# An attention-plus-MLP kernel on one core: prologue, load order and wave placement changed

## The chip, the cores and the metric

One Trainium2 chip, of which the program uses one core. The metric is device microseconds of one execution. Matmuls run on PE (TensorE); DVE (VectorE), ACT (ScalarE) and POOL (GpSimd) do the rest; SP (SyncE) issues most of the DMAs.

## The reference

Polynomial-sketch attention, and then an MLP with a swish whose slope is a parameter of each hidden unit. Batch 4, 4 heads, 1088 tokens, 32 numbers per head; r = 8, so a token has 64 features per head; 4352 tokens in all, d_model 128, d_ff 2048.

```python
def phi(x):
    a = np.einsum('rd,bhsd->bhsr', S1, x)
    b = np.einsum('rd,bhsd->bhsr', S2, x)
    return np.einsum('bhsi,bhsj->bhsij', a, b).reshape(*x.shape[:-1], r * r)
q_p, k_p = (phi(q), phi(k))
kv = np.einsum('bhsf,bhsd->bhfd', k_p, v)
z = np.sum(k_p, axis=2)
num = np.einsum('bhsf,bhfd->bhsd', q_p, kv)
den = np.einsum('bhsf,bhf->bhs', q_p, z)[..., None] + 1e-06
x = (num / den), heads side by side            # 4352 x 128
h = x @ w_in
g = h * (1.0 / (1.0 + np.exp(-beta * h)))
out = g @ w_out
```

## The kernel before

The kernel folds beta into the weights: `winp` is w_in times beta, `woutp` is w_out over beta, both in f16, so that the swish is a plain Silu on ACT. They are made on the chip: `scale_w_in` (POOL, eight pairs of 128-column blocks), `scale_w_out` (ACT, first half) and `scale_w_out_pool` (POOL, second half). `beta_rows` spreads beta over the partitions with matmuls against ones.

Each batch is an `Attention` object. Its steps: `k_turn` and `q_turn` (DVE 32x32 transposes of the loaded k and q, to kT and qT), `k_project` and `q_project` (PE, both sketches at once, then the DVE transposes back to `ab`), `k_product` (outer product of the two sketches, split between DVE and POOL), `v_copy`, `kv` (PE, key features against v with a column of ones, so z comes with it), `kv_spread`, `weights`, `kv_repeat` (layouts for the next products), `denominators`, `q_multiply` and `q_back` (query features of one third of the tokens, transposed to `qpt`), and `num` (PE, query features against kv, four token groups s on 32 rows each). Batch 0 divides after num (`num_first`, `spread_rden`, `rden_rows`, `quotient`); the others scale the query features first (`weigh`), and then `num_part` and `evacuate` write `xT`, the MLP's input in f16.

The MLP goes over three chunks of a batch (384, 384 and 320 columns), each in 8 waves. A wave is two matmuls with `winp` into a pair of PSUM banks, one Silu over both to `gT`, and, two waves later, the two matmuls of `second` with `woutp` that add to `acc`. So there are 24 waves per batch and 96 in all. After a chunk's last one the DVE transposes `acc` to `osb` and SP stores it.

The order on each engine is the order in which the code is written. A list of slots (`at_wave`) says behind which wave which attention step of the same or the next batch is issued. Every engine takes its instructions in that order, so an instruction that waits holds up what stands behind it. PSUM tiles come from three tags with two buffers each: `att` (a bank), `acc` (a bank), `wave` (a pair).

All loads are issued at the start of the program: k of batch 0 and beta from ACT's queue, the rest from SP's in the order S1, S2, q, v of batch 0, w_in, w_out, then k, v, q of batches 1, 2, 3. `warm(n)` issues n matmuls on zeros.

Of the kernel before, what the change touches and what calls it, by code (L numbers as in the profile page):

```python
# [13 lines left out]
P = 128  # L14
T = 32
# [3 lines left out]
def kernel(  # L19
# [61 lines left out]
    def load_v(b):  # L81
        for s in range(NS):
# [23 lines left out]
    load_v(0)  # L106
    nc.scalar.dma_start(out=betat, in_=moe_beta.rearrange("(p j) -> p j", j=NJ))
    nc.sync.dma_start(out=w_in_sb, in_=moe_w_in)
    nc.sync.dma_start(out=w_out_sb, in_=moe_w_out.rearrange("(p j) m -> p j m", j=NJ))
    for b in range(1, B):  # L110
        nc.sync.dma_start(out=k_in[b], in_=k_rows[b])
        load_v(b)
        nc.sync.dma_start(out=q_in[b], in_=q_rows[b])
# [109 lines left out]
    def scale_w_in():  # L223
        for j in range(0, NJ, 2):
# [25 lines left out]
    class Attention:  # L250
# [68 lines left out]
        def kv(self, r):  # L319

            if r == 0:
                self.kvp = bank("att")
            for c in range(C):
                for g in range(4):
                    h = 2 * r + g // 2
                    nc.tensor.matmul(  # L326
                        out=self.kvp[T * g : T * g + T, r * (D + 1) : (r + 1) * (D + 1)],
                        lhsT=self.kp[:, c * H + h, (g % 2) * T : (g % 2) * T + T],
                        rhs=self.vc[:, c, h, :],
                        start=(c == 0),  # L330
                        stop=(c == C - 1),
                    )

        def kv_spread(self):
            kvx = sb.tile([P, 4, 2, D], F32, tag="kvx", name="kvx")
            nc.vector.tensor_tensor(
                out=kvx,
# [344 lines left out]
```

## Time and profile before

| | us |
|---|---|
| three runs | 134.78, 133.62, 134.84; median 134.78 |
| the profiled execution | 135.82, of which the span is 134.1 |
| PE busy / weight loads | 113.0 / 62.0 |
| ACT busy | 83.5 |
| DVE busy | 69.4 |
| POOL busy | 29.8 |
| mean granted PE clock | 0.955 |
| DMA read / written | 8.80 MB / 2.23 MB |

The span runs from the first instruction to the last. The chain of waits is followed back from the last instruction, at each step to what released it; "issue" in it is time in which an engine waited for nothing that the profile shows. PE's busy time counts matmuls whose ends are modelled, so a busy PE need not be at its peak. In a row of the timeline stand start, duration, engine, line, operation, tiles, shapes and count, and in brackets the idle time before it with its releaser. The granted clock has records only from about 16 us on; before that the profile shows 1.00.

### The profile page before, as it was taken

To read this page: it belongs to the slowest core of one execution; us is meant where nothing else is said; L and a number is where in the kernel's file an instruction comes from. 1 tells how busy PE (TensorE), PEld (TensorE's weight loads), DVE (VectorE), ACT (ScalarE), POOL (GpSimd) and SP (SyncE) were. 2 spreads that over 40 slices of the span, in tenths; PEclk is the share of its full clock that TensorE was granted. 3 is DMA by queue.
4 is the path that set the end of the run, shared out by engine and by line. 5 is a ranking of instruction groups with operands and counts; after the bars stand their busy time and mean duration, and the time that the engine had idled before them with its cause. 6 is when DMAs were issued, how large, how long until landed. Compare 5 with 4: busy or idle time off the path is not lost.

```text
span 134.1 us, 4076 instructions
## 1 busy us (share of the span) xinstructions
PE 113.0 (84%) x1777; PEld 62.0 (46%) x1777; DVE 69.4 (52%) x131; ACT 83.5 (62%) x141; POOL 29.8 (22%) x48
## 2 busy tenths in 40 slices
PE   6986950579996999975999998999999899999940
PEld 2312530453643675643446644645574565555610
DVE  4429640338589312999950379988036991010110
ACT  1354210076753757864767786877878689999930
POOL 6205899910005700000191000008000000000000
PEclk9999999555999999999999999999999999999997
DMA  4999999999981210013300301321030031203222
GB/s 144 223 175 289 403 160 191 223 177 250 156 187 61 42 29 0 2 19 45 48 6 5 59 0 19 45 39 15 5 50 13 0 59 17 37 12 49 34 40 39
DMA packets 22122, 11.29 MB, mean 84 GB/s; under 512 B 18773, under 2 KB 20821, under 8 KB 21849
## 3 DMA queue, kind: packets, MB, share of 16 engines
q1 hardware_dynamic: 21808, 10.46, 39.3%
q10 hardware_dynamic: 296, 0.57, 1.3%
q8 instruction: 14, 0.23, 0.7%
q14 instruction: 4, 0.02, 0.1%
HBM read 8.80 MB, written 2.23 MB: 82 GB/s over the span
## 4 chain that ended last, share of the span: by engine, by line
PE 52%; DVE 20%; ACT 12%; DMA 6%; issue 5%; SPq 0%; DVEq 0%; ACTq 0%
PE wave L556 15%; ACT gT L559 11%; PE acc L536 11%; PE att L442 7%; DMA q_in<-in_q_dram 6%; PE att L326 5%; DVE qp L425 4%; DVE qpt L433 4%; PE att L286 3%; PE att L469 3%; PE att L381 3%; PE acc L180 2%; DVE qT L265 2%; PE att L366 2%; DVE kp L312 1%
## 5 line engine op out<-in xcount | busy, mean ns | idle before, releaser
L559 ACT ACTIVATE gT<-wave 128x768 f16<-128x768 f32 (+1 forms) x96 | 68.5, 775 | 21.5 <-PE wave L556 21.3
L556 PE MATMUL wave<-xT,winp 128*128 128x384 f16 (+1 forms) x192 | 46.2, 323 | 2.2 <-DVE xT L512 1.4
L536 PE MATMUL acc<-gT,woutp 128*128 128x384 f16 (+1 forms) x192 | 45.3, 318 | 0.2 <-ACT gT L559 0.2
L556 PEld LDWEIGHTS <-winp 128*128 128x128 f16 x192 | 16.6, 99 | 20.6 <-issue 10.0
L312 POOL TENSOR_TENSOR kp<-ab 128x768 f32<-128x768 f32 (+1 forms) x4 | 12.1, 3037 | 62.3 <-DVE ab L295 47.6
L536 PEld LDWEIGHTS <-woutp 128*128 128x128 f16 x192 | 18.7, 98 | 11.3 <-issue 0.7
L541 DVE STREAM_TRANSPOSE osb<-acc 128x384 f32<-128x384 f32 (+1 forms) x12 | 6.5, 540 | 24.5 <-PE acc L536 24.5
L442 PE MATMUL att<-qpt,kvw 32*32 32x96 f32 (+1 forms) x512 | 12.4, 277 | 2.2 <-DVE qpt L433 1.8
L433 DVE STREAM_TRANSPOSE qpt<-qp 128x768 f32<-128x768 f32 x12 | 11.7, 971 | 0.2
L442 PEld LDWEIGHTS att<-qpt,kvw 32*32 32x32 f32 x512 | 7.8, 104 | 7.2 <-DVE qpt L433 2.8
L381 PE MATMUL att<-qT,wc 128*32 128x288 f32 (+2 forms) x40 | 3.6, 409 | 5.8 <-issue 5.4
L425 DVE TENSOR_TENSOR qp<-an,ab 128x768 f32<-128x768 f32 x9 | 8.4, 930 | 0.1
L225 POOL TENSOR_TENSOR winp<-w_in_sb,beta_bc 128x256 f16<-128x256 f32 x8 | 8.3, 1074 | 0.5 <-DMA w_in_sb<-in_moe_w_in_dram 0.5
L390 DVE STREAM_TRANSPOSE cc<-att 128x288 f32<-128x288 f32 (+2 forms) x5 | 2.1, 423 | 12.0 <-PE att L381 12.0
L180 PE MATMUL acc<-idle 128*128 128x512 f16 x15 | 7.0, 629 | 1.3 <-DVE idle L117 1.3
L312 DVE TENSOR_TENSOR kp<-ab 128x1536 f32<-128x1536 f32 (+1 forms) x4 | 7.3, 1825 | 0.3
L295 DVE STREAM_TRANSPOSE ab<-att 128x288 f32<-128x288 f32 x16 | 6.7, 454 | 1.2 <-PE att L286 1.2
L326 PEld LDWEIGHTS att<-vc,kp 128*32 128x32 f32 x576 | 5.9, 113 | 2.7 <-issue 2.7
L286 PE MATMUL att<-qT,wab 64*32 64x288 f32 x64 | 4.3, 482 | 3.3 <-DVE ab L295 3.1
L265 DVE STREAM_TRANSPOSE qT<-q_in 128x1088 f32<-128x1088 f32 x4 | 5.1, 1279 | 3.1 <-DMA q_in<-in_q_dram 3.1
L326 PE MATMUL att<-vc,kp 128*32 128x33 f32 x576 | 6.7, 202 | 0.0
L490 ACT COPY ns<-wave 128x192 f32<-128x192 f32 x2 | 0.6, 319 | 7.6 <-PE wave L442 7.6
(71 smaller groups left out, 81.6 us busy)
## 6 DMA issues: line engine op xcount, KB each, us to landing
q_in<-in_q_dram SPq DMA_DIRECT2D x4, 544.0 KB, 8.7
v_in<-in_v_dram SPq DMA_DIRECT2D x12, 144.0 KB, 10.7
k_in<-in_k_dram SPq DMA_DIRECT2D x3, 544.0 KB, 14.4
out_dram<-osb SPq DMA_DIRECT2D x32, 48.0 KB, 1.9
w_in_sb<-in_moe_w_in_dram SPq DMA_DIRECT2D x1, 1024.0 KB
w_out_sb<-in_moe_w_out_dram SPq DMA_DIRECT2D x1, 1024.0 KB, 9.2
out_dram<-osb SPq DMA_DIRECT2D x16, 40.0 KB, 1.7
k_in<-in_k_dram ACTq DMA_DIRECT2D x1, 544.0 KB, 3.9
```

The lines of the kernel that those rows point to most:

```text
L180: nc.tensor.matmul(out=w, lhsT=idle[:, 0:P], rhs=idle, start=True, stop=True)
L225: nc.gpsimd.tensor_tensor(out=winp[:, j : j + 2, :], in0=apx(w_in_sb, j, [[1, 2], [NJ, P]]), in1=apx(beta_bc, j, [[1, 2], [NJ, P]]), op=AL ...
L265: nc.vector.transpose(out=self.qT[:, 0:U, :].rearrange("p u t -> p (u t)"), in_=q_in[self.b])
L286: nc.tensor.matmul(out=banks[p][T * s : T * s + T, 0 : C * T], lhsT=wab[64 * p : 64 * p + 64, :], rhs=apx(src[64 * p : 64 * p + 64], s * s ...
L312: eng.tensor_tensor(out=apx(self.kp, c0 * H * F, [[F, n], [R, R], [1, R]]), in0=apx(t, c0 * H * 2 * R, [[2 * R, n], [1, R], [0, R]]), in1= ...
L326: nc.tensor.matmul(out=self.kvp[T * g : T * g + T, r * (D + 1) : (r + 1) * (D + 1)], lhsT=self.kp[:, c * H + h, (g % 2) * T : (g % 2) * T ...
L425: nc.vector.tensor_tensor(out=apx(self.qp, 0, [[F, n], [R, R], [1, R]]), in0=a, in1=apx(self.ab, c0 * H * 2 * R + R, [[2 * R, n], [0, R], ...
L433: nc.vector.transpose(out=apx(self.qpt, ch * CW * T, [[T, CW], [C * T, 2 * H], [1, T]]), in_=self.qp.rearrange("p n f -> p (n f)"),)
L442: nc.tensor.matmul(out=dst[T * h : T * h + T, 0:n], lhsT=self.kvw[T * s : T * s + T, (h % 2) * 2 + fb, h // 2, :], rhs=self.qpt[T * s : T ...
L536: nc.tensor.matmul(out=acc[:, :n], lhsT=woutp[:, j, :], rhs=gT[:, j, :n], start=(j == 0), stop=(j == NJ - 1))
L556: nc.tensor.matmul(out=wave[:, jj, :n], lhsT=winp[:, j, :], rhs=x[:, :n], start=True, stop=True)
L559: nc.scalar.activation(out=gT[:, 2 * w : 2 * w + 2, :n], in_=wave[:, :, :n], func=ACTF.Silu)
```

## The change

The prologue is written in another order, with twelve idle matmuls ahead of the attention's products instead of fifteen in other places, two after `kv` and two after the first quotient. Loads other than k, q and the small ones of batch 0 are held: a memset of the target's first column, placed in the program of POOL or the DVE, must have run before SP may issue the load. w_in is held by the DVE behind the turn of k, w_out behind the k product, batch 1 by POOL between its scalings, batches 2 and 3 by the DVE 19 (k, q) and 14 (v) waves ahead of their batch's first slot wave. In batch 0 `kv` uses 64 columns at a time with its two head pairs in separate banks, half of v's copy goes from ACT to POOL, and the second and third chunk's num, denominators' rows and quotient are done together. `num` takes two token groups in turn: its matmuls alternate between two groups of 32 rows and two banks. All of w_out's scaling is on POOL, in turn with the second half of w_in's. The slots have other wave numbers.

```diff
     def load_v(b):
-        for s in range(NS):
+        for s in (0, 2, 1, 3):
...
+    def hold(eng, t):
+        eng.memset(t[:, 0:1], 0.0)
+
+    def load_w_in(eng):
+        hold(eng, w_in_sb)
+        nc.sync.dma_start(out=w_in_sb, in_=moe_w_in)
+        nc.sync.dma_start(out=betat, in_=moe_beta.rearrange("(p j) -> p j", j=NJ))
...
+    load_v_late(0, nc.gpsimd)
...
-                parts = ((nc.scalar.copy, 0, 2), (nc.scalar.copy, 2, H))
+                parts = ((nc.scalar.copy, 0, 2), (nc.gpsimd.tensor_copy, 2, H))
...
+            if self.first:
+                parts = [(nc.vector, 0, 4), (nc.vector, 4, 7), (nc.gpsimd, 7, C)]
+            else:
+                parts = [(nc.gpsimd, 6, C), (nc.vector, 0, 6)]
...
+            m = F if self.first else T
             for c in range(C):
...
+                for r in rs:
+                    for g in range(2 * F // m):
+                        h = 2 * r + g * m // F
+                        f0 = g * m % F
+                        nc.tensor.matmul(
+                            out=self.kvp[m * g : m * g + m, r * self.kvs : r * self.kvs + D + 1],
+                            lhsT=self.kp[:, c * H + h, f0 : f0 + m],
...
-        def num(self, s, dst, c0, c1):
+        def num(self, s0, banks, c0, c1):
+
             n = (c1 - c0) * T
             for fb in range(2):
                 for h in range(H):
...
+                    for i, dst in enumerate(banks):
+                        s = s0 + i
+                        nc.tensor.matmul(
+                            out=dst[T * h : T * h + T, 0:n],
+                            lhsT=self.kvw[T * s : T * s + T, (h % 2) * 2 + fb, h // 2, :],
...
+        def rden_rows(self, ch0, ch1):
+
+            banks = [bank("att") for _ in range(ch0, ch1)]
+            for i, w in enumerate(banks):
+                for s in range(NS):
...
+    warm(9)
+    a0.k_turn((0,))
+    sketches()
+    warm(2)
+    a0.k_turn((1,))
+    load_w_in(nc.vector)
+    a0.k_project()
+    a0.q_turn()
+    beta_rows()
+    warm(1)
+    a0.v_copy()
+    a0.k_product()
+    load_w_out(nc.vector)
+    a0.q_project()
+    a0.kv((0, 1))
     a0.q_multiply(0)
     a0.kv_spread()
-    a0.q_back(0)
+    warm(2)
     a0.weights()
     a0.kv_repeat()
+    a0.q_back(0)
+    nc.vector.reciprocal(out=rbetat, in_=betat)
     a0.denominators(0, 1, rz[:, 0:CW, 0:H])
-    a0.num_first(0, "wave")
+    scale_w_in(0, 4)
+    load_k(1, nc.gpsimd)
+    scale_w_in(4, 8)
+    load_q(1, nc.gpsimd)
+    a0.num_first(0, 1)
     a0.spread_rden(0, 1)
-    scale_w_out(0, NJ // 2)
-    a0.quotient(0)
-    scale_w_out_pool(NJ // 2, NJ)
+    a0.quotient(0, 1)
+    warm(2)
+    scale_w_out(0, 2)
+    load_v_late(1, nc.gpsimd)
+    for j in range(8, NJ, 2):
+        scale_w_in(j, j + 2)
+        scale_w_out(j - 6, j - 4)
+    scale_w_out(NJ - 6, NJ)
...
+            turn_k, turn_q, proj_k, proj_q, kv0, kv1, wt, den, n0, n1, n2, n3 = 0, 2, 2, 5, 7, 8, 10, 11, 18, 20, 25, 28
```

Three places show what stands in a row now. First the DVE in the prologue, from the S products to the projection of q. kT and qT are the turned k and q of batch 0, ab a projection turned back (k's, then q's), kp the k product. Before:

```order
L195 TENSOR_TENSOR wab<-att,hmask 128x32
L259 STREAM_TRANSPOSE kT_130<-k_in_70 128x576
L259 STREAM_TRANSPOSE kT_130<-k_in_70 128x512
L265 STREAM_TRANSPOSE qT_132<-q_in_66 128x1088
L574 TENSOR_REDUCE rep_161<-ident 128x32
L295 STREAM_TRANSPOSE ab<-att 128x9x32 x2
L312 TENSOR_TENSOR kp<-ab 128x1792
L295 STREAM_TRANSPOSE ab<-att 128x9x32 x2
```

The same stretch of the DVE's order after the change:

```order
L600 TENSOR_REDUCE rep_141<-ident 128x32
L277 STREAM_TRANSPOSE kT_105<-k_in_70 128x576
L218 TENSOR_TENSOR wab<-att,hmask 128x32
L277 STREAM_TRANSPOSE kT_105<-k_in_70 128x512
L109 MEMSET w_in_sb 128x1
L313 STREAM_TRANSPOSE ab<-att 128x9x32 x2
L283 STREAM_TRANSPOSE qT_107<-q_in_66 128x1088
L333 TENSOR_TENSOR kp<-ab 128x1024
L333 TENSOR_TENSOR kp<-ab 128x768
L109 MEMSET w_out_sb 128x1
L313 STREAM_TRANSPOSE ab<-att 128x9x32 x2
```

The turn of q has moved behind the first ab, and the memsets that hold w_in and w_out stand in the row.

Second, PE from kv to the first wave. Before:

```order
L326 MATMUL att<-vc_148,kp 32x33 x72
L351 MATMUL att<-zi,s2rep 128x32
L366 MATMUL att<-kvx,rep 128x256
L381 MATMUL att<-qT_132,wc 32x96 x4
L442 MATMUL wave<-qpt,kvw 32x96 x32
L469 MATMUL att<-rzt,sel_164 128x96 x4
L556 LDWEIGHTS winp
L556 MATMUL wave<-xT,winp 128x384
```

PE's order over the same steps after the change, with the idle matmuls that stand among them:

```order
L352 MATMUL wave<-vc_128,kp 64x33 x36
L203 LDWEIGHTS idle
L203 MATMUL acc<-idle 128x512
L203 LDWEIGHTS idle
L203 MATMUL acc<-idle 128x512
L376 MATMUL att<-zi,s2rep 128x32
L391 MATMUL att<-kvx,rep 128x256
L406 MATMUL att<-qT_107,wc 32x96 x4
L470 MATMUL wave<-qpt,kvw 32x96 x32
L496 MATMUL att<-rzt,sel_144 128x96 x4
```

kv has half the matmuls, each twice as wide; the steps behind it are the same, with idle matmuls ahead of `weights` and, not shown, two between the last row and the first wave.

Third, the DVE in batch 0's first waves, from the first chunk's xT on. Before:

```order
L498 TENSOR_TENSOR xT<-att,ns 128x384
L425 TENSOR_TENSOR qp<-ab 128x768
L433 STREAM_TRANSPOSE qpt<-qp 128x3x8x32
L390 STREAM_TRANSPOSE cc<-att 128x192
L392 TENSOR_TENSOR prod_154<-ab,cc 128x24x8
L399 TENSOR_REDUCE den<-prod_154 128x24
L400 RECIPROCAL rz<-den 128x6x4
L462 STREAM_TRANSPOSE rzt<-rz 128x192
L259 STREAM_TRANSPOSE kT_134<-k_in_71 128x576
L259 STREAM_TRANSPOSE kT_134<-k_in_71 128x512
L498 TENSOR_TENSOR xT<-att,ns 128x384
```

After, from the last step of the denominators on (the second and third chunk's qp and qpt stand ahead of them):

```order
L489 STREAM_TRANSPOSE rzt<-rz 128x192
L277 STREAM_TRANSPOSE kT_109<-k_in_71 128x576
L277 STREAM_TRANSPOSE kT_109<-k_in_71 128x512
L283 STREAM_TRANSPOSE qT_111<-q_in_67 128x1088
L313 STREAM_TRANSPOSE ab<-att 128x9x32 x2
L333 TENSOR_TENSOR kp<-ab 128x1536
L109 MEMSET k_in_72 128x1
L109 MEMSET q_in_68 128x1
L527 TENSOR_TENSOR xT<-att,ns 128x384 x2
L313 STREAM_TRANSPOSE ab<-att 128x9x32 x2
```

The second chunk's xT has moved behind batch 1's turn of q, projection and k product, and comes together with the third's.

More of the change, by code (lines that the diff above doesn't have):

```diff
@@ L460, in spread_rden @@
             self.rzt = sb.tile([P, 2 * CT], F32, tag="rzt", name="rzt")
-            self.rz0 = ch0
             nc.vector.transpose(out=self.rzt[:, 0:n], in_=apx(rz, ch0 * CT, [[1, n]]))
-        def rden_rows(self, ch):
-            w = bank("att")
-            for s in range(NS):
-                o = (ch - self.rz0) * CT
-                nc.tensor.matmul(
-                    out=w[:, s * CT : (s + 1) * CT],
-                    lhsT=sel4[:, s, :, :].rearrange("p h d -> p (h d)"),
-                    rhs=self.rzt[:, o : o + CT],
-                    start=True,
-                    stop=True,
-                )
-            return w
@@ L478, in num_first @@
-        def num_first(self, ch, tag):
-            self.ns = sb.tile([P, NS, CT], F32, tag="ns", name="ns")
-            for s0 in (0, 2):
-                if tag == "wave":
-                    w = pair()
-                    banks = [w[:, 0, :], w[:, 1, :]]
-                else:
-                    banks = [bank(tag), bank(tag)]
-                for i in range(2):
-                    self.num(s0 + i, banks[i], ch * CW, (ch + 1) * CW)
-                if tag == "wave":
-                    nc.scalar.copy(out=self.ns[:, s0 : s0 + 2, :], in_=w[:, :, 0:CT])
-                else:
-                    for i in range(2):
-                        nc.scalar.copy(out=self.ns[:, s0 + i, :], in_=banks[i][:, 0:CT])
@@ new lines, in num_first @@
+        def num_first(self, ch0, ch1):
+            n = (ch1 - ch0) * CT
+            self.ns = sb.tile([P, 2, NS, CT], F32, tag="ns", name="ns")
+            for s0 in (0, 2):
+                if ch0 == 0:
+                    w = pair()
+                    self.num(s0, [w[:, i, :] for i in range(2)], 0, ch1 * CW)
+                    nc.scalar.copy(out=self.ns[:, 0, s0 : s0 + 2, :], in_=w[:, :, 0:CT])
+                else:
+                    banks = [bank("att"), bank("att")]
+                    self.num(s0, banks, ch0 * CW, ch1 * CW)
+                    for i in range(2):
+                        nc.scalar.copy(
+                            out=self.ns[:, 0 : ch1 - ch0, s0 + i, :],
+                            in_=banks[i][:, 0:n].rearrange("p (c n) -> p c n", n=CT),
+                        )
@@ L502, in num_part, with quotient @@
+        def quotient(self, ch0, ch1):
+            banks = self.rden_rows(ch0, ch1)
+            x = self.xt()
+            for i, w in enumerate(banks):
+                nc.vector.tensor_tensor(
+                    out=x[:, ch0 + i, :],
+                    in0=w[:, 0:NMAX],
+                    in1=self.ns[:, i, :, :].rearrange("p s n -> p (s n)"),
+                    op=ALU.mult,
+                )
         def num_part(self, s0, ch0, ch1):
@@ L504, in num_part @@
             banks = [bank("att"), bank("att")]
-            for i in range(2):
-                self.num(s0 + i, banks[i], ch0 * CW, ch1 * CW)
+            self.num(s0, banks, ch0 * CW, ch1 * CW)
             self.parts = (s0, ch0, ch1, banks)
@@ L640 @@
+        for i, w in enumerate((n2, n3)):
+            at_wave(
+                w0 + w,
                 lambda a=a, i=i: a.num_part(2 * i, 1, NCH),
```

161 lines of the change are left out of this document (70 added, 91 removed).

## The prediction

> **What bounds the kernel now.** A measurement of this kernel tells about 1% from no change. I read the chain of waits first, then the same execution cut into five stages. The stages start at the first instruction and at waves 1, 25, 49 and 73 (a wave is two 384-column matmuls of the first MLP product; 24 waves make a batch). Columns: window, length, busy us of PE, PE weight loads, DVE, ACT and POOL, granted clock, DMA share, GB/s.
>
> ```profile
> 0.00:29.83 29.83, 19.17 (x293) 9.04 (x294) 12.39 (x31) 9.25 (x22) 18.10 (x41) 0.89 0.96 221
> 29.83:61.89 32.06, 28.13 (x496) 16.17 (x496) 21.37 (x39) 19.68 (x34) 4.31 (x3) 0.95 0.41 82
> 61.89:86.24 24.35, 23.52 (x412) 13.27 (x413) 16.62 (x30) 17.90 (x29) 4.31 (x3) 1.00 0.18 28
> 86.24:110.17 23.93, 23.43 (x413) 13.11 (x412) 16.38 (x30) 18.69 (x30) 3.08 (x1) 1.00 0.17 25
> 110.17:134.10 23.93, 18.70 (x165) 10.45 (x163) 2.66 (x5) 17.99 (x29) 0.00 (x0) 0.96 0.21 32
> ```
>
> Batches 1 and 2 keep PE busy for 97% of their time and take about 24 us each; batch 0 needs 32 us for the same number of waves; 29.8 us pass before the first wave. So the prologue and batch 0 hold what can be won. The chain in the prologue:
>
> ```profile
> 1.58 7.72 DMA q_in<-in_q_dram
> 9.33 1.31 DVE qT L265
> ...
> 11.33 1.57 PE att L286 x16
> ...
> 19.71 5.39 issue
> ...
> 25.41 1.75 PE wave L442 x57
> 27.16 1.96 PE att L469 x8
> ...
> 29.83 1.44 PE wave L556 x4
> ```
>
> Three things stand out: the k path waits for q (the DVE turns q, L265, before it takes k's projection, L295); PE stops for 5.39 us between two matmuls of one loop with nothing to wait for; and what follows is slow. The DMA view of 19.7 to 22.3 us, and then of 22.3 to 23.8 us, shows what the stop is:
>
> ```profile
> q1 hardware_dynamic: 262, 0.42, 103.2%
> ```
> ```profile
> q8 instruction: 1, 0.02, 5.8%
> ```
>
> In the stop the data queue fills all engines with loads of later batches, and the one instruction packet moves only in the second window; PE runs again at 25.1 (19.71 + 5.39). I read it as PE's next instructions arriving late. The clock follows:
>
> ```profile
> 20.00:23.40 3.40, 0.00 (x0) 0.00 (x0) 0.00 (x0) 0.00 (x0) 3.40 (x4) 0.94 1.06 186
> 23.40:26.80 3.40, 1.71 (x64) 1.42 (x64) 1.21 (x5) 0.32 (x1) 3.32 (x7) 0.50 1.04 227
> 30.10:33.50 3.40, 3.40 (x18) 1.27 (x17) 2.78 (x6) 2.15 (x3) 0.00 (x0) 0.53 1.07 249
> ```
>
> After the stop PE is granted half its clock until about 33 us.
>
> **The change, part by part.** The prologue's terms, in the order of time:
>
> ```profile
> 1.26 2.74 PE L180 MATMUL acc<-idle 128*128 128x512 f16 x6 [1.26 <-DVE idle L117]
> 4.53 1.23 PE L216 MATMUL wave<-beta,ones 1*128 1x512 f32 x3
> 4.83 1.36 DVE L259 STREAM_TRANSPOSE kT<-k_in 128x576 f32<-128x576 f32 x2
> 6.95 1.21 PE L286 MATMUL att<-kT,wab 64*32 64x288 f32 x16
> 10.81 0.83 DVE L295 STREAM_TRANSPOSE ab<-att 128x288 f32<-128x288 f32 x2
> 11.68 2.03 DVE L312 TENSOR_TENSOR kp<-ab 128x1792 f32<-128x1792 f32 x1
> 11.72 2.90 POOL L312 TENSOR_TENSOR kp<-ab 128x512 f32<-128x512 f32 x1 [7.12 <-DVE ab L295]
> 12.86 1.43 ACT L276 COPY vc<-v_in 128x448 f32<-128x448 f32 x4 [1.12 <-DMA v_in<-in_v_dram]
> 15.17 8.29 POOL L225 TENSOR_TENSOR winp<-w_in_sb,beta_bc 128x256 f16<-128x256 f32 x8 [0.54 <-DMA w_in_sb<-in_moe_w_in_dram]
> 17.32 0.42 DVE L336 TENSOR_TENSOR kvx<-att,bmask 128x256 f32<-128x256 f32 x1 [1.86 <-PE att L326]
> ```
>
> Six idle matmuls took 2.74 us, 0.46 each; nine end at 1.26 + 4.1 = 5.4. The S products lay between the end of the old six (4.0) and the beta rows (4.53): 0.5. With two more idle ones it is 6.8, and k's projection at the old 1.21 ends at 8.0 (kT, 1.36 from about 4.8, is ready). The idle matmuls lie in time that PE spent waiting; uncovered, each would cost its 0.46. Now the DVE takes ab at once: 0.83, to 8.9; then the turn of q, 1.31, to 10.2; then the k product, now in two pieces, 2.03 and 0.1 for the extra start, to 12.3. It was 13.7 before.
>
> PE meanwhile: the beta rows took from 4.53 to 6.95, 2.4, so to 10.4; one idle matmul; q's projection at the old 1.57 (the chain's row), to 12.5. The DVE now has ab of q (0.83) and qp (0.95) ahead of kvx: 14.3.
>
> On POOL its two chunks of the k product now stand behind half of v's copy. v lands when k, q and v (1.67 MB) are through: at the stage's 221 GB/s, 7.6 us, begun at about 2, so at 10 by an estimate. Half of the old ACT copy, 0.7, and 2.90 end at 13.6. Of the outer products (L326), half the instructions at twice the width, most are done by then; kv ends at about 14.1, level with the DVE. So kvx stands at 14.4 against 17.32, 2.9 earlier.
>
> From kvx to the first wave it was 29.83 - 17.32 = 12.51. The stop takes 5.39 of it. The half clock takes about half of the two PE pieces, 1.75 and 1.96; the second has a row at full clock:
>
> ```profile
> 36.19 1.03 PE L469 MATMUL att<-rzt,sel 128*128 128x96 f32 x8
> ```
>
> That is 0.9 + 0.9. What stays is 5.3. I add 0.8 for beta's reciprocal, which now stands in this chain, and for hand-overs between engines: first wave at 20.5, **9.3 us earlier**. Bounds: 18.5 if the projections and the beta rows run at half their durations and v lands at 9; 22.5 if v lands at 12.
>
> The Trainium skill ("TensorE: Matmul & The Clock Gate", Part 1) says that the default is half clock and that a busy window of some 3.4 us frees it, so nearly gapless idle matmuls from 1.3 us on should free it by about 8 us; by that the first wave would come near 19. The trace agrees on the loss (0.50 after the stop); I take the slow durations.
>
> Holding the loads adds one-column memsets (single columns, far below the rows here) and puts waits on SP: behind w_in's wait stand w_out and all of batch 1, which nothing needs earlier. POOL then owns all of w_out's scaling: eight pairs of w_in at 1.04 us (8.29 / 8) from 13.6 on, with four pairs of w_out between them that cost no more than that: the last w_in pair is ready by 26.1, and wave 8 needs it near 30. If that cover goes (v 4 us late), each microsecond counts in full. ACT loses its half of the scaling, which lay ahead of its first silu and in no chain: nothing.
>
> Batch 0. The rows that carry it:
>
> ```profile
> L433 DVE STREAM_TRANSPOSE qpt<-qp 128x768 f32<-128x768 f32 x12 | 11.7, 971 | 0.2
> L425 DVE TENSOR_TENSOR qp<-ab 128x768 f32<-128x768 f32 x3 | 2.8, 945 | 0.0
> L312 DVE TENSOR_TENSOR kp<-ab 128x1536 f32<-128x1536 f32 x3 | 5.3, 1758 | 0.3
> L498 DVE TENSOR_TENSOR xT<-att,ns 128x384 f16<-128x384 f32 x3 | 1.7, 558 | 7.1 <-PE att L469 7.1
> 32.13 0.38 DVE L390 STREAM_TRANSPOSE cc<-att 128x192 f32<-128x192 f32 x1 [0.48 <-PE att L381]
> 33.70 0.38 DVE L462 STREAM_TRANSPOSE rzt<-rz 128x192 f32<-128x192 f32 x1
> 43.99 1.79 PE att L442 x64
> 58.20 0.59 PE L442 MATMUL att<-qpt,kvw 32*32 32x96 f32 x32 [0.79 <-DVE qpt L433]
> 61.89 0.50 PE L556 MATMUL wave<-xT,winp 128*128 128x384 f16 x2 [1.39 <-DVE xT L512]
> 42.38 0.50 PE L556 MATMUL wave<-xT,winp 128*128 128x384 f16 x2
> ```
>
> Wave 9 (the second chunk) started at 42.38. In the new order the DVE sets it: two qp and two qpt (3.8), the denominators' five steps (32.13 to 34.08: 1.95), kT 1.36, qT 1.31, ab 0.83, kp 1.76, two xT 1.1: 12.1. PE's projection of q needs the two banks that xT frees, 1.0: 13.1 after the first wave, against 12.55 before, which had the slow clock but one chunk less. From there to batch 1's first wave it was 19.51; the second num_first and rden (1.79 + 1.03) have moved ahead and the two stalls (0.79, 1.39) go, because batch 1's denominators now stand eight waves ahead of the first num, not six: 14.5. Batch 0 is 27.6, and with 0.2 for one more wait of PE behind its bank 27.8, **4.3 us less**. Bounds 25.5 (PE's 28.13 busy us less 1.7 for the slow clock and 0.9 for num) and 32 (the DVE late again).
>
> Batches 1 and 2: the denominators move one wave ahead, which covers the stall of this row, and num alternates its row groups:
>
> ```profile
> 106.11 0.59 PE L442 MATMUL att<-qpt,kvw 32*32 32x96 f32 x32 [0.50 <-DVE qpt L433]
> 113.73 0.91 PE L442 MATMUL att<-qpt,kvw 32*32 32x192 f32 x32
> ```
>
> A batch has two of each: 3.0 us of num. The trace has no alternating 32-row matmul; the bounds are nothing and half of it, 1.5; I take 0.6, nearer to nothing, since 18 ns per 96-column record leave little beside issue. With the stall, 1.1 per batch, **2.2 us**. Batch 3 stays: in its stage ACT is busy 17.99 us with nothing of a next batch to move, and the rest is the way out.
>
> Sum: 9.3 + 4.3 + 2.2 = 15.8. The profiled execution took 135.82 (span 134.1), one above the median 134.78 of the three timed; the three lie within 0.9% of each other, so each must hold these waits, and I take the gain off the median: 119.0.
>
> **Rivals.** (a) The stop isn't cured. By the Trainium skill ("Runtime: NRT & Kernel Launch", Instruction fetch mechanics) instructions come in 16 KiB blocks, fetched while the block before runs, so that crossing costs almost nothing; by that the 5.39 us is something else and stays. The 0.02 MB packet that moves just before PE resumes speaks for the fetch; that other such packets cause no stop, for the page. The new kv drops 72 matmul records and num_first and rden add 72 ahead of the first wave, so the same count of instructions is reached right there, where k, q and v of batch 1 are loading. Price: 5.4 and some 2 of slow clock: 126.5. (b) The DVE chain keeps batch 0 at 32 us: 119.0 + 4.3 = 123.3; for it speaks that this chain, with 12.1 us in a row, has no slack; against it, that the stalls were at full DVE load. (c) Slower than before: the loads of batches 2 and 3 now start in waves 6 and 30 instead of being done by 42 us, so a late fetch can strike again in each stretch of full DMA. Each stop costs 5.4 plus about 3 of half clock, 8.4; the gain of 15.8 is gone with two of them, and three give 119.0 + 25.2 = 144. Against it: in batches 1 and 2, with PE 97% busy and DMA at 18%, the trace has no such stop. (d) Full clock and num halved: 119.0 - 1.5 - 1.8 = 115.7.
>
> **How the numbers follow.** Forecast, 117 to 122: 0.52. (b) and part stops, 122 to 125: 0.18. (a): 0.13. (d) and below: 0.12. (c): 0.03; ends near the old time by a mix of a and b: 0.02. The range from 115.5 to 126 leaves out half of (a), (c) and the lower end of (d), under 2 in 10. Faster 0.95, same 0.02, slower 0.03.
>
> **What would show it.** First wave at 20.5 and no issue wait of PE over 1 us before it or in waves 1 to 8; clock 1.0 from about 10 us; the k product before the end of q's projection; wave 9 at about 33.6, then batch 1 at 48; num rows of 0.91 down to about 0.7; batches 1 and 2 at 23. I'm wrong if a stop of 5 us returns, if wave 9 comes later than 16 us after the first, or if POOL's weights are late.

## The result, and the profile after

The changed kernel takes 123.65 us (median of four runs, 122.31 to 124.97) against 134.6 for the kernel before (four runs, 133.62 to 134.84). The ratio is 0.917, with a 95% interval of 0.907 to 0.926. The forecast was 119.0 with a range of 115.5 to 126: the direction and the range held, and of the 15.8 us expected 10.95 came. The profiled execution, 124.97 with a span of 123.1, is the longest of the four and the ratio leaves it out; its span is 11.0 shorter than the 134.1 of before, which is nearly the difference of the medians, so its stages serve to say where the time lies.

The stages of the changed kernel, cut at the same waves (1, 25, 49, 73). The columns are window, length, busy us of PE, PE weight loads, DVE, ACT and POOL, granted clock, DMA share, GB/s:

```profile
0.00:24.98 24.98, 19.33 (x222) 10.93 (x223) 17.48 (x34) 6.16 (x12) 14.47 (x43) 0.74 0.73 220
24.98:53.73 28.75, 27.45 (x433) 15.20 (x432) 22.85 (x42) 18.16 (x29) 12.19 (x12) 0.93 0.28 74
53.73:76.61 22.88, 22.88 (x414) 12.80 (x413) 16.63 (x33) 18.44 (x30) 4.61 (x3) 1.00 0.40 101
76.61:99.52 22.91, 22.91 (x414) 12.80 (x413) 16.38 (x30) 18.47 (x30) 3.08 (x1) 1.00 0.18 27
99.52:123.10 23.58, 18.81 (x165) 10.35 (x163) 2.58 (x5) 17.97 (x29) 0.00 (x0) 0.96 0.21 32
```

| stage | before | after | gained | forecast |
|---|---|---|---|---|
| to the first wave | 29.83 | 24.98 | 4.85 | 9.3 |
| batch 0 | 32.06 | 28.75 | 3.31 | 4.3 |
| batch 1 | 24.35 | 22.88 | 1.47 | 1.1 |
| batch 2 | 23.93 | 22.91 | 1.02 | 1.1 |
| batch 3 and the way out | 23.93 | 23.58 | 0.35 | 0 |

The prologue holds nearly all of what is missing. Its chain of waits, in order of time, has no PE stop any more, but one DVE product that stands out:

```profile
12.16 3.47 DVE qp L450
15.63 2.29 issue
```

The "issue" behind qp is no late instruction: in the DVE's timeline qp itself lasts to 18.0, and kvx stands behind it.

```profile
12.16 5.84 DVE L450 TENSOR_TENSOR qp<-ab 128x768 f32<-128x768 f32 x1
17.92 0.41 DVE L362 TENSOR_TENSOR kvx<-wave,bmask 128x256 f32<-128x256 f32 x1
```

POOL's timeline over the same time: its piece of the k product and four pairs of w_in's scaling, one behind the other without a gap, to 17.18.

```profile
11.98 1.06 POOL L333 TENSOR_TENSOR kp<-ab 128x512 f32<-128x512 f32 x1
13.01 2.12 POOL L248 TENSOR_TENSOR winp<-w_in_sb,beta_bc 128x256 f16<-128x256 f32 x2
15.13 2.05 POOL L248 TENSOR_TENSOR winp<-w_in_sb,beta_bc 128x256 f16<-128x256 f32 x2
```

PE had been done with kv for two microseconds by then, and from 12.0 on all its steps ran at half the clock (kv's 68 records 3.73, rden's eight matmuls 2.02 where a row of before has 1.03):

```profile
11.83 3.73 PE L352 MATMUL wave<-vc,kp 128*64 128x33 f32 x68 [0.35 <-POOL vc L294]
18.57 0.61 PE L376 MATMUL att<-zi,s2rep 128*128 128x32 f32 x2 [2.04 <-DVE zi L369]
22.24 2.02 PE L496 MATMUL att<-rzt,sel 128*128 128x96 f32 x8
```

The windows between the changes of the granted clock (the third column from the right):

```profile
5.20:8.60 3.40, 3.35 (x38) 1.27 (x37) 2.36 (x7) 0.61 (x2) 0.00 (x0) 1.00 1.02 239
8.60:12.00 3.40, 1.20 (x26) 0.58 (x27) 3.40 (x6) 2.35 (x4) 1.47 (x3) 1.00 0.91 294
12.00:25.60 13.60, 11.46 (x159) 8.19 (x158) 10.14 (x14) 1.01 (x3) 10.31 (x16) 0.50 0.64 202
32.40:35.90 3.50, 3.50 (x25) 1.28 (x24) 2.71 (x5) 1.78 (x4) 0.21 (x1) 0.51 0.00 0
```

The idle matmuls did free the clock, at 5.2, as the Trainium skill ("TensorE: Matmul & The Clock Gate", Part 1) let one expect; here the trace agrees (the same first nine did not free it before 13.7 in five later profiles). But in the 3.4 us from 8.6 on PE was busy for only 1.20, waiting for the DVE, and from 12.0 to 25.6 the clock was at half again.

### The profile page after: what moved, and what is told of

It reads as the page before. It is cut to its first block, busy times and chain, and to the rows that moved or that the text cites. A ratio compares the mean times of both kernels' runs of the same rounds, so it can differ in the third digit from the quotient of the medians.

```text
span 123.1 us, 3822 instructions
## 1 busy us (share of the span) xinstructions
PE 111.4 (90%) x1642; PEld 62.1 (50%) x1642; DVE 75.9 (62%) x140; ACT 79.2 (64%) x127; POOL 34.4 (28%) x58
## 4 chain that ended last, share of the span: by engine, by line
PE 69%; DVE 13%; ACT 11%; issue 3%; DVEq 0%
PE wave L587 22%; PE acc L567 19%; ACT gT L590 10%; PE att L470 8%; DVE qp L450 5%; PE att L304 4%; PE att L352 4%; PE acc L203 4%; PE att L496 3%; PE att L391 2%; PE att L406 2%; DVE kp L333 2%; DVE qpt L458 2%; DVE qT L283 1%; DVE ab L313 1%
## 5 line engine op out<-in xcount | busy, mean ns | idle before, releaser
L333 POOL TENSOR_TENSOR kp<-ab 128x768 f32<-128x768 f32 (+1 forms) x4 | 10.3, 2576 | 16.7 <-DVE ab L313 16.7
L294 POOL COPY vc<-v_in 128x896 f32<-128x896 f32 (+3 forms) x8 | 6.3, 815 | 28.7 <-DMA v_in<-in_v_dram 17.5
L470 PE MATMUL att<-qpt,kvw 32*32 32x192 f32 (+1 forms) x448 | 10.9, 293 | 0.7 <-ACT ns L518 0.4
L470 PEld LDWEIGHTS att<-qpt,kvw 32*32 32x32 f32 x448 | 6.2, 104 | 5.2 <-DVE qpt L458 1.5
L450 DVE TENSOR_TENSOR qp<-ab 128x768 f32<-128x768 f32 x3 | 8.6, 2874 | 0.0
L399 ACT COPY kvw<-att 128x256 f32<-128x256 f32 x4 | 1.5, 372 | 9.4 <-PE att L391 9.2
L333 DVE TENSOR_TENSOR kp<-ab 128x1536 f32<-128x1536 f32 (+2 forms) x5 | 7.3, 1481 | 0.2
L257 POOL TENSOR_TENSOR woutp<-w_out_sb,rbetat 128x256 f16<-128x256 f32 x8 | 6.5, 824 | 3.3 <-DVE rbetat L624 3.3
L277 DVE STREAM_TRANSPOSE kT<-k_in 128x576 f32<-128x576 f32 (+1 forms) x8 | 5.5, 711 | 1.7 <-DMA k_in<-in_k_dram 1.7
L352 PEld LDWEIGHTS att<-vc,kp 128*32 128x32 f32 x432 | 4.3, 109 | 1.9 <-issue 1.9
```

What stands on the lines that cost most here:

```text
L333: eng.tensor_tensor(out=apx(self.kp, c0 * H * F, [[F, n], [R, R], [1, R]]), in0=apx(t, c0 * H * 2 * R, [[2 * R, n], [1, R], [0, R]]), in1= ...
L352: nc.tensor.matmul(out=self.kvp[m * g : m * g + m, r * self.kvs : r * self.kvs + D + 1], lhsT=self.kp[:, c * H + h, f0 : f0 + m], rhs=self ...
L450: nc.vector.tensor_tensor(out=apx(self.qp, 0, [[F, n], [R, R], [1, R]]), in0=a, in1=apx(self.ab, c0 * H * 2 * R + R, [[2 * R, n], [0, R], ...
L470: nc.tensor.matmul(out=dst[T * h : T * h + T, 0:n], lhsT=self.kvw[T * s : T * s + T, (h % 2) * 2 + fb, h // 2, :], rhs=self.qpt[T * s : T ...
```

## The experiments

Three theories stood for the prologue. A: POOL's row of work keeps the DVE from its qp product, which was priced (0.95) by a row of before in which it did not wait for POOL. B: the clock, lost from 12.0 on, stretches everything from kv to the first wave. C: the stop of before was a late instruction fetch, and holding the loads cured it. For the rest it had to be found which part of the change gave the gain of batches 0 to 2.

**POOL waits for qp** (on the changed kernel):

```diff
     a0.denominators(0, 1, rz[:, 0:CW, 0:H])
+    seen = const.tile([P, 1], F32, tag="seen")
+    nc.gpsimd.tensor_copy(out=seen, in_=a0.qp[:, 0, 0:1])
     scale_w_in(0, 4)
```

> One tiny POOL copy that reads the first query product (qp) stands ahead of POOL's weight scaling, so that the scaling can't run beside qp; nothing else differs from the changed kernel. Theory A (qp takes 5.84 us because POOL works through the w_in scaling at the same time): qp falls to 1 to 2 us, kvx starts at the end of kv, about 15.7 instead of 17.9, the first wave at about 22.7 instead of 25.0, and the time falls by about 2 us, to 121.5. Theory B (qp is long for another reason, such as the loads that land in SBUF or a wait that the record hides): qp stays above 4 us and the time within 1 us of 123.6.

Measured: 122.45 us, median of four (118.85 to 123.75), 1.2 under the changed kernel's median, with spreads that overlap. The DVE's timeline:

```profile
13.48 1.20 DVE L450 TENSOR_TENSOR qp<-ab 128x768 f32<-128x768 f32 x1
16.85 0.42 DVE L362 TENSOR_TENSOR kvx<-wave,bmask 128x256 f32<-128x256 f32 x1 [2.17 <-PE wave L352]
```

qp took 1.20 in place of 5.84, and kvx now waits for kv, not for the DVE. So POOL's work is what held qp: that is shown. Only the fastest of the four lies below every run of the changed kernel, and the median gains little; in the profiled execution kv, at half clock, ends only at 16.7, and the first wave came at 23.93.

**More idle matmuls** (on the changed kernel), to keep the clock:

```diff
     beta_rows()
-    warm(1)
+    warm(6)
...
     a0.q_project()
+    warm(4)
     a0.kv((0, 1))
```

> The changed kernel with six idle matmuls instead of one ahead of q's projection and four more ahead of kv, in the two gaps of about 1 us where PE waited. Clock theory (the clock is lost at 12.0 us because of these gaps): it stays 1.0 at least to 15 us and kv, 3.7 us for its last 68 records before, takes under 2.2 and ends at about 13.4. By theory A the DVE's qp still holds kvx to about 17.9, so PE idles from 13.5 to 18.5, and the time moves by less than 1 us. Rival (the gaps have nothing to do with it): clock 0.5 from 12 us on as in the changed kernel, kv at 3.7 us.

Measured: 124.49 (122.43 to 124.56), no gain. Here the first idle matmuls did not free the clock; it came at 13.7, and the five added ones, at half clock themselves, pushed q's projection back to 12.8. qp, still beside POOL's row, took 3.91, and kvx started at 18.79:

```profile
14.95 3.91 DVE L450 TENSOR_TENSOR qp<-ab 128x768 f32<-128x768 f32 x1
```

**Both edits together** (the two diffs above):

> Both edits together: POOL's scaling behind qp, and the gaps ahead of q's projection and of kv filled with idle matmuls. If both theories hold, kv ends at about 13.4, kvx starts by 14.2, the 8 rden records take about 1.0 us instead of 2.0, the first wave starts at 19.5 to 20.5 and the time is 118 to 119.5: the two gain more together (about 5 us) than one by one (2 and under 1). If only theory A holds: as with the POOL edit alone, 121.5. If neither: 123.6.

Measured: 122.37 (118.45 to 122.85). Only the best of four runs met the expected time. In its profile (122.0) both causes are gone, and the first wave still starts only at 23.24:

```profile
14.92 2.29 PE L352 MATMUL wave<-vc,kp 128*64 128x33 f32 x72
15.02 0.96 DVE L450 TENSOR_TENSOR qp<-ab 128x768 f32<-128x768 f32 x1
21.39 1.13 PE L496 MATMUL att<-rzt,sel 128*128 128x96 f32 x8 [0.77 <-DVE rzt L489]
23.24 0.81 PE L587 MATMUL wave<-xT,winp 128*128 128x384 f16 x4 [0.28 <-DVE xT L527]
```

kvx stood at 17.33 here, so from kvx to the first wave it was 5.9 at full clock, against 7.06 in the changed kernel at half. That puts a price of some 1.2 on the clock in this piece. The rest of the lateness is q's projection, which started at 12.8 behind six idle matmuls (at 9.53 in the changed kernel, at 10.66 with POOL waiting alone). kv began at 14.92 here against 12.68 there: the added idle matmuls took back most of what the clock gave.

**Idle matmuls earlier instead, and POOL waits** (the wait of the first experiment, and):

```diff
     sketches()
-    warm(2)
+    warm(5)
     a0.k_turn((1,))
```

> The changed kernel with POOL's scaling behind qp, as in the first experiment, and five instead of two idle matmuls between the S products and k's projection. If dense idle matmuls over two of the clock's steps of 3.4 us are what frees it, it is free by 8.2 us in most executions, where it was free before 10 us in only 2 of 8 profiles of the changed order; then the median falls from 122.4 of the first experiment to about 120. If k's projection, which comes up to 1.2 us later, costs more than the clock gives: 122 to 123.

Measured: 122.02 (121.11 to 124.19), ratio to the kernel before 0.913 (0.896 to 0.931): the expected 120 was missed. qp took 1.20, the first wave came at 22.31, and the clock was lost again:

```profile
10.61 4.03 PE L352 MATMUL wave<-vc,kp 128*64 128x33 f32 x72 [0.53 <-ACT vc L294]
10.80:24.40 13.60, 12.79 (x166) 8.98 (x164) 8.90 (x18) 2.27 (x5) 12.72 (x18) 0.50 0.66 211
```

From 10.8 to 24.4 PE counted as busy for 12.79 of 13.6 us and stayed at half clock. So a PE that is busy with kv's 33-column matmuls and the small float32 products behind it did not get the clock back; what the clock goes by can't be read from busy time.

**No holds** (on the changed kernel, `hold` returns at once), to test C:

```diff
     def hold(eng, t):
-        eng.memset(t[:, 0:1], 0.0)
+        return
```

> The changed kernel without the memsets that hold the loads, so that SP issues them as early as it can; all else the same. Fetch theory (PE's next instructions come late while the loads fill the DMA engines): an issue wait of PE of 3 to 6 us shows again after about 450 PE records, which is at the first wave, the clock is lost behind it, and the time rises by 4 to 8 us, to 128 to 131. Rival (the stop had another cause, and the new order alone removed it): no issue wait above 1 us, time within 1 us of 123.6.

Measured: 124.17 (122.24 to 125.39), ratio to the kernel before 0.914 (0.900 to 0.928): the same as the changed kernel, and no stop, though DMA was as full as before. The DMA view of 13 to 16 us, and then of 16 to 19 us (packets, MB, share of 16 engines):

```profile
q1 hardware_dynamic: 239, 1.22, 98.8%
```
```profile
q1 hardware_dynamic: 517, 0.90, 103.3%
q8 instruction: 1, 0.02, 2.2%
```

The instruction packet moved through full engines, from 16.4 on. So in the new order the holds aren't needed against the stop, and my expectation fell; the kernel with kv as it was, below, shows why. qp was stretched here too, by the same row of POOL's work:

```profile
13.47 5.23 DVE L450 TENSOR_TENSOR qp<-ab 128x768 f32<-128x768 f32 x1
```

This run has the same half clock to the first wave (25.69) as the one in which POOL waits (23.93); the 1.8 between them is what A costs when kv is slow as well.

**The count of instructions shifted** (on the kernel before: sixteen idle matmuls of 32 columns behind the first six):

```diff
     warm(6)
+    w = bank("acc")
+    for _ in range(16):
+        nc.tensor.matmul(out=w[:, 0:32], lhsT=idle[:, 0:P], rhs=idle[:, 0:32], start=True, stop=True)
```

> The kernel before with 16 more idle matmuls of only 32 columns behind its first six, so that 32 more PE instructions precede everything else; they lie where PE waits. Fetch theory (PE stops where its next block of instructions is not there yet): the stop of about 5 us stays, but 16 matmuls earlier in the program: no longer at the eighth denominators' matmul (L381) but inside kv (L326), about 5 matmuls before its end. Rival (something that this very matmul waits for and the profile doesn't show): the stop stays at the eighth L381 record.

Measured: 137.33 (one run; the kernel before on that chip 135.11). The stop moved from the last matmul of the denominators' first product forward into kv. PE's timeline of this kernel:

```profile
14.45 1.47 PE L326 MATMUL att<-vc,kp 128*32 128x33 f32 x140
21.43 0.33 PE L326 MATMUL att<-vc,kp 128*32 128x33 f32 x4 [5.51 <-issue]
```

The windows from the start to the stop's end, of this kernel and then of the kernel before, hold nearly the same number of PE records (the figures in brackets behind PE and its weight loads):

```profile
0.00:21.40 21.40, 11.95 (x221) 4.98 (x222) 8.98 (x20) 5.93 (x11) 13.90 (x34) 0.91 0.93 281
```
```profile
0.00:25.05 25.05, 15.15 (x220) 5.80 (x221) 10.47 (x24) 6.30 (x12) 16.06 (x38) 0.96 0.94 231
```

The stop goes with the count of instructions and not with the step or its operands. It is PE waiting for its next instructions: shown, and the instruction packets, below, agree. The Trainium skill ("Runtime: NRT & Kernel Launch", Instruction fetch mechanics) has such a crossing mostly hidden; here the trace differs, it cost 5.51 us.

**Holds alone** (on the kernel before, loads of batches 1 to 3 held, all else as it was):

```diff
+    def load(b, eng):
+        for t in (k_in[b], v_in[b].rearrange("p h c d -> p (h c d)"), q_in[b]):
+            eng.memset(t[:, 0:1], 0.0)
         nc.sync.dma_start(out=k_in[b], in_=k_rows[b])
...
     scale_w_in()
+    load(1, nc.gpsimd)
...
+    at_wave(5, lambda: load(2, nc.vector))
+    at_wave(29, lambda: load(3, nc.vector))
```

> The kernel before with the loads of batches 1 to 3 held by one-column memsets (batch 1 behind POOL's w_in scaling, batches 2 and 3 by the DVE at waves 5 and 29), and nothing else of the change. If the full DMA engines delay PE's instructions, they are idle from about 17 us on and the stop falls below 1 us; the first wave comes near 24.5 instead of 29.8, and the time near 129 if batch 1's later loads cost nothing. The run of the changed kernel without holds speaks against it: there the DMA engines were full and no stop came. Then the stop stays at 4 us or more.

Measured: 130.63 (one run, against 135.11). PE's timeline has no stop ahead of the first wave (one of 0.84 came in batch 0), and that wave came at 23.93:

```profile
20.12 0.37 PE L384 MATMUL att<-qT,wc 128*32 128x96 f32 x8 [0.46 <-ACT kvw L377]
23.93 1.19 PE L559 MATMUL wave<-xT,winp 128*128 128x384 f16 x4 [0.72 <-DVE xT L501]
```

From 16 to 19 us the data queue held 1.4% of the DMA engines' time. The old prologue with idle DMA engines is thus 1 us earlier than the changed kernel's 24.98. The cure of the stop alone is worth more than the 4.85 that the prologue gained (29.83 - 23.93 = 5.9, in a run that had the full clock from 17.4, late in kv, to the first wave); the rest of the new prologue, as it ran in the profiled execution, gave 1.05 of it back. With DMA full, the old order stops; with DMA idle, it doesn't; the new order, with kv at 64 columns, doesn't in either case.

**Only the order of the loads** (on the kernel before):

```diff
-        for s in range(NS):
+        for s in (0, 2, 1, 3):
...
-        load_v(b)
         nc.sync.dma_start(out=q_in[b], in_=q_rows[b])
+        load_v(b)
```

> The kernel before with only the order of its loads as in the changed one (v's four pieces as 0, 2, 1, 3; q ahead of v in batches 1 to 3), with no holds. The changed kernel without holds had no stop although its DMA engines were full; if the order of the loads is why, PE's stop of 5 us goes here too, and the first wave comes near 24.5 us. If the stop stays at 3 us or more, it isn't the order of the loads.

Measured: 133.26 (one run; the kernel before on that chip 135.22, 133.08 to 137.95). The stop came before the same matmul and was shorter:

```profile
21.56 0.32 PE L381 MATMUL att<-qT,wc 128*32 128x96 f32 x1 [3.22 <-issue]
```

That says little for the order of the loads, since another kernel below, with the old order, had 3.94.

**No holds, and kv as it was** (the edit to `hold`, and kv at 32 columns in one bank, one head pair behind the other):

```diff
-                self.kvp = pair().rearrange("p r n -> p (r n)") if self.first else bank("att")
-                self.kvs = 512 if self.first else D + 1
-            m = F if self.first else T
+                self.kvp = bank("att")
+                self.kvs = D + 1
+            m = T
...
-    a0.kv((0, 1))
+    a0.kv((0,))
+    a0.kv((1,))
```

> The changed kernel without holds and with batch 0's kv back at 32 columns at a time, one head pair after the other in one bank: 72 more matmuls and weight loads, as before. If the narrow kv made the stop (PE goes through 288 instructions in under 2 us, so that the next block is needed sooner), it returns here: an issue wait of 2 us or more between kv and the first wave. If neither the holds nor kv's width matter and the order of the prologue alone does: none above 1 us.

Measured: 122.91 (one run). The first wave came at 21.71, the earliest of all. Yet the stop is there again, short: num waits 0.97 at 18.84, and no operand explains it (the DVE's cc, named as its releaser, is none of them, and qpt and kvw had been written by 17.8). It comes after the same 220 matmuls and 221 weight loads as in the kernel before. PE's row, that of its weight loads, and the window up to it; then the window to the same count in the kernel without holds:

```profile
18.84 0.98 PE L470 MATMUL wave<-qpt,kvw 32*32 32x96 f32 x64 [0.97 <-DVE cc L415]
18.85 0.77 PEld L470 LDWEIGHTS wave<-qpt,kvw 32*32 32x32 f32 x63 [0.89 <-issue]
0.00:18.80 18.80, 13.01 (x220) 6.19 (x221) 12.21 (x27) 5.53 (x10) 10.62 (x35) 0.82 0.91 279
0.00:24.70 24.70, 20.98 (x220) 11.12 (x221) 16.50 (x30) 6.05 (x12) 13.53 (x38) 1.00 0.84 267
```

This settles what the new order does. In the five kernels with a stop ahead of the first wave PE went on 2.6 to 3.0 us after the instruction packet began to move: at 25.09 after 22.3 in the kernel before, at 18.84 after 16.0 here. Without holds the packet moved at 16.4, but PE needed what it brings only at 24.7, because kv has 72 matmuls fewer and the count falls behind rden; with the narrow kv it falls ahead of num, at 17.9, which is too early. With holds alone the packet moved at 17.1, 3.3 ahead of the count. What sets the time of the packet (12.0 to 22.3 in these traces) stays open.

Another stop, of 1.51, came in batch 1 (inside kv, to 61.85). qp was short, without any wait written into POOL's program: it waited for the end of POOL's k piece (13.48), and the DVE got its turn ahead of the scaling.

```profile
12.58 1.71 DVE L450 TENSOR_TENSOR qp<-ab 128x768 f32<-128x768 f32 x1
```

The window over kv of this kernel, and kv in PE's timeline of the kernel before:

```profile
12.30:15.00 2.70, 2.47 (x145) 2.29 (x146) 1.96 (x2) 0.00 (x0) 2.55 (x3) 0.50 1.03 421
```
```profile
15.51 1.70 PE L326 MATMUL att<-vc,kp 128*32 128x33 f32 x144
```

kv at 32 columns takes some 2.4 us at half clock (2.47 with an idle matmul's start) and 1.70 at full; at 64 columns it takes 3.73 (68 of its 72 records) to 4.03 at half and 2.29 at full (the rows above). So half the matmuls at twice the width are dearer, by 0.6 us at full clock and by about 1.5 at half: 12 and 17 ns a record against 32 and 55.

**A meeting made on purpose** (on the kernel before; the one-column copy stands ahead of qp on the DVE), so that qp starts inside POOL's row:

```diff
-    scale_w_in()
+    scale_w_in(0, 2)
+    seen = const.tile([P, 1], F32, tag="seen")
+    nc.vector.tensor_copy(out=seen, in_=winp[:, 0, 0:1])
+    scale_w_in(2, NJ)
```

> The kernel before with one tiny DVE copy, ahead of qp, of the first scaled pair of w_in, so that qp starts while POOL works through the other seven pairs without a gap; before, qp ran ahead of them in 0.94 us. Lock theory (the DVE's product of two SBUF operands gets no turn while POOL's scalings follow each other): qp lasts until POOL's row of pairs ends, 4 to 7 us, and the first wave comes later or at the same time as the stop allows. Rival (they share the memory at a lower rate): qp takes 1.2 to 2 us.

Measured: 133.5 (one run). In the DVE's and POOL's timelines:

```profile
15.02 1.63 DVE L425 TENSOR_TENSOR qp<-ab 128x768 f32<-128x768 f32 x1
```
```profile
13.69 8.88 POOL L225 TENSOR_TENSOR winp<-w_in_sb,beta_bc 128x256 f16<-128x256 f32 x8
```

qp waited some 0.7 and then ran, with six pairs still to come. My expectation that a row of POOL's keeps the DVE out until it ends fell. It was kept out for the row in the changed kernel, without holds (5.23), with more idle matmuls (3.91) and with the old slots below (5.26), and for one instruction here and in the run before. With the holds alone and with the loads reordered qp began 0.07 ahead of POOL's row and took 0.94. Who gets the next turn when the row has begun is open.

**The old slots** (on the changed kernel, the steps at the old wave numbers; for batch 1 and the others):

```diff
-            turn_k, turn_q, proj_k, proj_q, kv0, kv1, wt, den, n0, n1, n2, n3 = 3, 4, 5, 7, 8, 10, 11, 11, 19, 21, 24, 28
+            turn_k, turn_q, proj_k, proj_q, kv0, kv1, wt, den, n0, n1, n2, n3 = 3, 4, 5, 7, 11, 12, 14, 15, 21, 23, 28, 30
...
-            turn_k, turn_q, proj_k, proj_q, kv0, kv1, wt, den, n0, n1, n2, n3 = 0, 2, 2, 5, 7, 8, 10, 11, 18, 20, 25, 28
+            turn_k, turn_q, proj_k, proj_q, kv0, kv1, wt, den, n0, n1, n2, n3 = 0, 1, 2, 4, 8, 9, 11, 12, 18, 20, 25, 27
```

> The changed kernel with the old wave numbers for batches 1 to 3 (batch 1: 3, 4, 5, 7, 11, 12, 14, 15, 21, 23, 28, 30; batches 2 and 3: 0, 1, 2, 4, 8, 9, 11, 12, 18, 20, 25, 27). If the placement carries the gain of batches 1 and 2: their stages go from 22.9 back to 23.7 to 24.2 us each, and batch 0's from 28.7 to about 30.5, with PE waiting for the DVE ahead of num and of batch 1's first wave. If num's alternation carries it: 22.9 stays.

Measured: 129.78 (one run). Its stages for batches 0, 1 and 2:

```profile
25.74:56.08 30.34, 26.77 (x433) 14.93 (x432) 22.76 (x42) 18.58 (x29) 11.70 (x12) 1.00 0.26 68
56.08:80.66 24.58, 23.54 (x413) 13.17 (x413) 16.60 (x33) 17.90 (x29) 4.37 (x3) 1.00 0.39 96
80.66:104.53 23.87, 23.37 (x413) 12.93 (x412) 16.38 (x30) 18.50 (x30) 3.08 (x1) 1.00 0.17 26
```

And the two stalls at the end of batch 0, which the new slots had removed, are there again:

```profile
52.38 0.56 PE L470 MATMUL att<-qpt,kvw 32*32 32x96 f32 x32 [1.18 <-DVE qpt L458]
56.08 0.50 PE L587 MATMUL wave<-xT,winp 128*128 128x384 f16 x2 [1.45 <-DVE xT L543]
```

Against the kernel without holds, whose first wave (25.69) came as late and whose stages are 27.94, 23.23 and 22.91, the slots are worth 2.4, 1.35 and 0.96: 4.7 us.

**num one group after the other** (on the changed kernel):

```diff
-            for fb in range(2):
-                for h in range(H):
-                    for i, dst in enumerate(banks):
-                        s = s0 + i
+            for i, dst in enumerate(banks):
+                s = s0 + i
+                for fb in range(2):
+                    for h in range(H):
```

> The changed kernel with num's matmuls for one token group after the other, as before. The traces have 0.59 and 0.91 us for a num of 96 and 192 columns before and 0.56 and 0.88 after: if alternation is worth that and no more, the rows go back to 0.59 and 0.91 and the stages of batches 1 and 2 lengthen by about 0.12 us each. My forecast's term of 0.6 us per batch would show as 23.5.

Measured: 121.23 (one run). The rows of num, and those of the changed kernel behind them:

```profile
68.89 0.59 PE L470 MATMUL att<-qpt,kvw 32*32 32x96 f32 x32
74.27 0.91 PE L470 MATMUL att<-qpt,kvw 32*32 32x192 f32 x32
```
```profile
72.60 0.56 PE L470 MATMUL att<-qpt,kvw 32*32 32x96 f32 x32
81.54 0.88 PE L470 MATMUL att<-qpt,kvw 32*32 32x192 f32 x32
```

Alternating saves 0.03 in each, 0.12 in a batch. The stages of batches 1 and 2 agree: 22.98 and 23.02 against 22.88 and 22.91. This run was faster as a whole because its prologue and batch 0 were: qp took 1.20 although nothing held POOL off, the first wave came at 22.25, and the clock was whole from 22.8 on.

```profile
12.47 1.20 DVE L450 TENSOR_TENSOR qp<-ab 128x768 f32<-128x768 f32 x1
22.25:49.97 27.72, 26.67 (x434) 15.01 (x433) 22.62 (x42) 18.25 (x29) 12.07 (x12) 0.99 0.32 84
```

No version is clearly better than the changed kernel: the medians of those run four times lie between 122.0 and 124.5, each with a spread of some 2 to 5 us. Holds, POOL's wait and kv at 32 columns together were not run.

## Why the prediction was right, and where it was not

**The stop goes: right, for half the reason.** It was instruction fetch (the shift of the count shows it), and holding the loads cures it (holds alone). But the new order doesn't stop without the holds either. Rival (a) had the place right, the same count just ahead of the first wave, and (a) did not happen because PE gets there 4 to 5 us later than before (at 24.0, without holds at 24.7, against 19.7), long after the packet (15.8 and 16.4); the prediction did not weigh that time. Nor did (c).

**The k path: right.** The k product ended at 11.35 (forecast 12.3), q's projection at 10.25 (12.5, priced at half clock) and v's last piece stood ready at about 10.5 (10). The first two were on the safe side by 1 to 2 us, with the clock's help: at half clock, with POOL waiting, they came at 12.7 and 11.9. The 2.90 for POOL's piece of the k product was also priced by a neighbour: in the trace of before it ran beside the DVE's product; behind it, in the changed kernel, it took 1.06. Copying half of v took POOL 1.48 instead of 0.7.

**The failed step** is "The DVE now has ab of q (0.83) and qp (0.95) ahead of kvx: 14.3". kvx started at 17.92: 3.5 of the 4.65 us that the forecast was too good. qp was priced by a row in which it did not have to wait for POOL. The order shows qp beside the scaling of w_in; what it can't show is that POOL would start that row at 13.0, right behind its k piece, while qp, started at 12.16, waited. The prediction's own terms already overlap, the scaling "from 13.6 on" and qp up to 14.3, and the meeting was put at nothing. With POOL's scaling held off, qp takes 0.96 to 1.20. The Trainium skill ("SBUF — State Buffer", SBUF: two separate sides) has the rule that was missed: a DVE operation with two SBUF inputs and a GpSimd operation that reads SBUF exclude each other, and the one that starts second is blocked until the other instruction has ended. The runs agree that it is blocked. They differ on how long: 5.84 is the rest of POOL's row of five instructions, not of one, while 1.63 and 1.71 are about one.

Behind it stands a second mis-sized term, "most are done by then; kv ends at about 14.1": it ended at 15.56. Without qp in the way kvx could have stood at about 15.7, so 2.2 of the 3.5 are qp's and 1.3 kv's. I had priced the wider kv as a saving; it is dearer, by some 1.5 at the half clock that it met. With kv begun 1.5 later at half clock (12.68 against 11.17), this is why holding POOL off alone moved little.

**From kvx to the first wave, "5.3 ... I add 0.8": right at full clock.** 6.1 was forecast; 5.9 was measured where the clock was granted (both edits), 7.06 in the changed kernel, 7.1 with POOL waiting. I had taken the slow durations ahead of kvx and the full clock behind it; the trace had it the other way round. That is the last 1.0 of the prologue's miss.

**Batch 0, 27.8: right without the slow clock.** It took 28.75 in the profiled execution, of which 3.5 us were at half clock (32.4 to 35.9), and 27.72 in the run with num serial, with the clock at 0.99 (28.06 with both edits, at 1.00). Wave 9 came 14.1 after the first wave (39.10) and 13.0 where the clock was whole (35.28 in the run with num serial), against the 13.1 summed up over the DVE's steps. Rival (b), the DVE chain keeping batch 0 at 32, fell. The two stalls went with the slots and came back with the old ones.

**Batches 1 and 2, 2.2: right as a sum (2.5), for another reason.** Of the 0.6 per batch given to num's alternation 0.12 is there, near the lower bound of nothing; the slots bring 1.35 and 0.96 where 0.5 was forecast for the one stall.

**POOL's weights were in time**, as forecast; the first w_out scaling waited for beta's reciprocal, behind qp on the DVE, to 20.5, and the one wait on PE's side that is put down to woutp, of a weight load ahead of the first wave, was 0.28.

The base was well chosen: medians and profiled spans differ by nearly the same, 10.95 and 11.0.

**The range held, in part by luck.** 123.65 lies outside the 117 to 122 of the main forecast, in the 122 to 125 given to rival (b) and part stops, and neither of these happened. Of the signs named, the missing stop and batches 1 and 2 at 23 came; the clock of 1.0 from 10 us on, the k product ahead of the end of q's projection (11.35 against 10.25), and num's rows of 0.7 (0.88) did not.

## What to carry to other kernels

When a step moves, look at what the *other* engine does at its new time: a price from a row of before holds only beside the neighbours it had there, and for DVE products of two SBUF operands the neighbour to look for is POOL. A stop of PE that no wait explains is tested by shifting the count of instructions: if it moves with the count, look when the instruction packet moves and when PE reaches that count; free DMA engines can bring the first forward, and fewer matmuls ahead of it put the second back. A rebuilt prologue should be tried in its parts: here the cure of the stop and the new slots, two small edits, gave 4.5 and 4.7 us, each by one run and one on the old kernel, the other on the new; by that estimate under 2 of the 10.95 are left for everything else. Halving the number of matmuls is no gain by itself; compare ns per record before and after.

## What the runs showed of the hardware

- The clock's history differs between executions whose prologue starts alike: freed at 5.2 in the changed kernel, at 13.7 and 13.9 in the two with more idle matmuls, at 4.0 in the run with five of them ahead of k's projection (and before these five began, at 5.15), and not before 27 us without holds, with the old slots and with POOL waiting. (Ahead of its first record the profile shows 1.00; there the durations tell: an idle matmul of 512 columns takes 0.46 at half clock.) Changes come on a grid of 3.4 us. This spreads the times of these kernels by some microseconds and limits what a prologue edit can be credited with.
- Half clock lasted 13.6 us, four steps of that grid, in the changed kernel and with the earlier idle matmuls, with PE busy for 11.46 and 12.79 of them, for the most part on small float32 products.
- A float32 matmul of 33 columns with weights of 64 columns cost 32 ns at full and 55 at half clock, with weights of 32 columns 12 and 17: more than twice for twice the width.
- In five kernels PE stopped after 441 to 443 records, matmuls and weight loads together, and went on 2.6 to 3.0 us after a packet of the instruction queue had begun to move; where that packet came 3.3 us or more ahead of the count, there was no stop.
- Alternating between two groups of 32 rows gave 3 to 5% (0.91 to 0.88, 0.59 to 0.56) for float32 matmuls of 192 and 96 columns.
